# Re-sorting the order list of a one-core attention and spectral-filter kernel by about 700 single moves

## The chip, the cores and the metric

The kernel runs on one core of one Trainium2 chip. The metric is the device time in microseconds (us), lower is better; with one core it is that core's time. The kernel before took 243.63 us at the median of three runs (242.74 to 247.04).

A profile is one recorded execution. Its span is about 2 us shorter than the time of the same run. The array's clock is in the records as a "granted clock", as a share of full speed.

## The reference, cut to what matters

```python
x = A_x                                        # 1 x 2048 x 640, bf16
g = sigmoid((x * gate_w).sum(-1, keepdims=True))
a = A_ref(x, wq, wk, wv, wo, beta)             # memory-augmented attention
b = irfft2(rfft2(x) * (w_r + 1j * w_i))        # spectral filter
out = g * a + (1 - g) * b

# A_ref: 32 heads of 20; 4 segments of 512 tokens, one after the other
for s in range(4):
    p = softmax(qs @ ks.T * scale + causal_mask)
    a_dot = p @ vs
    a_mem = phi(qs) @ M / (phi(qs) @ z + 1e-6)   # memory of earlier segments
    o = sigmoid(beta) * a_mem + (1 - sigmoid(beta)) * a_dot
    M, z = M + phi(ks).T @ vs, z + phi(ks).sum()
# phi(t) = t + 1 where t > 0, else exp(t)
```

## The kernel before

The program is recorded first and ordered second. Every matmul group, vector instruction and DMA is one operation with a number, the operations that it depends on, and the engines that may do it. A hand-tuned list then says in what order the operations stand and, where there is a choice, which engine takes each: value v means operation v // 2 on its engine number v % 2.

```python
def schedule(self, pools, order, nsem=56):
    ...
    for v in order:
        o = ops[v // 2]
        o.eng = list(o.alts)[v % 2]
        queue[o.eng].append(o)
    ...
        # inside head(e): when may the first operation of engine e start?
        if e == "dve" and o.lock:
            t = max(t, free["pool"])
        elif e == "pool":
            t = max(t, port)
```

All that reaches the chip is one queue per engine, in that order, and the semaphores between them. The small simulation in `schedule` only decides which PSUM bank and which semaphore each operation gets. The two branches at the end are its model of how VectorE ("dve") and GpSimd ("pool") hold each other up, with a time called `port`: in the simulation a VectorE operation recorded with `lock` waits until the GpSimd operation in flight is done.

An operation that either VectorE or GpSimd can do is recorded with both costs in nanoseconds (n elements per partition), and the sum of the spectral branch, called `W_add` here, is one of them:

```python
def either(self, fn, n, r, w, prio, name="", after=()):
    return self.Sc.op({"dve": (fn, 67 + 0.52 * n, 68.0), "pool": (fn, 120 + 1.95 * n, 50.0)}, ..., lock=True)

for r, (a0, a1, op) in enumerate(((0, 3, ALU.subtract), (1, 2, ALU.add))):
    fn = lambda e, ...: e.tensor_tensor(Yt.ap(...), Pt.ap(a0 * 322, ...), Pt.ap(a1 * 322, ...), op)
    self.either(fn, KD, ..., name="W_add")          # KD = 321
```

`warm_up` records ten matmuls of 512 columns on a tile of zeros, whose results nothing uses. `phi_max` and `phi_min` make the feature map phi on VectorE. `addmem` (128x640) adds the transposed memory part to the output in the tail and may go to either engine. `m_mask` and the causal masks run on GpSimd. The list of before begins like this:

```python
ORDER = (
    46, 0, 90, 26, 74, 23, 2, 4, 36, 24, 6, 8, 28, 10, 12, 72, 14, 16, 30, 18, 20, 178, ...
    ...            # 2328 entries; 2, 4, ... 20 are the ten warm-ups
)
```

Of the kernel before, what the change touches and what calls it, by code (L numbers as in the profile page):

```python
# [461 lines left out]
class Kern:  # L462
# [79 lines left out]
    def dma(self, dst, src, nbytes, r, w, prio, tr=False, name="", after=(), queue="sp"):  # L542
# [37 lines left out]
        46, 0, 90, 26, 74, 23, 2, 4, 36, 24, 6, 8, 28, 10, 12, 72, 14, 16, 30, 18, 20, 178, 64, 34, 202, 66, 68, 44, 42, 70, 93, 214, 52, 190, 48, 94,  # L580
        204, 97, 216, 180, 192, 218, 104, 98, 182, 76, 206, 101, 194, 38, 208, 220, 196, 103, 198, 222, 201, 184, 224, 186, 210, 188, 296, 50, 212,
        256, 298, 362, 78, 300, 536, 32, 80, 274, 538, 258, 83, 302, 260, 262, 276, 130, 278, 264, 84, 54, 280, 106, 266, 282, 1904, 86, 304, 364,
        284, 88, 366, 108, 380, 306, 576, 132, 826, 268, 290, 828, 814, 110, 368, 578, 831, 816, 113, 382, 384, 386, 819, 370, 540, 388, 832, 270,
        834, 410, 412, 272, 836, 414, 416, 391, 418, 552, 372, 490, 420, 288, 492, 494, 114, 496, 498, 554, 118, 820, 822, 134, 336, 500, 240, 137,
        338, 242, 340, 120, 348, 58, 824, 342, 116, 350, 308, 122, 312, 544, 142, 226, 932, 546, 124, 344, 292, 244, 56, 228, 144, 246, 286, 248, 347,
        139, 352, 230, 294, 232, 126, 250, 354, 146, 234, 374, 1906, 149, 237, 1908, 356, 254, 1910, 359, 2094, 151, 238, 1912, 844, 1914, 252, 2124,
        140, 2126, 1916, 2128, 128, 2130, 360, 166, 2096, 40, 846, 2098, 154, 2132, 848, 2100, 2134, 1924, 326, 1926, 314, 2102, 168, 392, 1928, 2104,
        1930, 156, 892, 310, 1932, 152, 838, 1944, 1934, 170, 334, 1946, 158, 894, 840, 324, 316, 1948, 842, 808, 897, 161, 328, 810, 1950, 1952, 394,
        320, 813, 880, 886, 163, 882, 322, 1954, 888, 560, 332, 502, 884, 504, 396, 506, 330, 172, 508, 890, 448, 376, 510, 1936, 398, 450, 436, 512,
        438, 378, 402, 452, 514, 562, 440, 174, 442, 2162, 400, 1962, 2164, 176, 444, 2166, 516, 556, 454, 456, 2168, 446, 165, 2170, 458, 464, 460,  # L590
        466, 406, 1918, 468, 462, 470, 570, 472, 408, 2172, 910, 912, 542, 474, 898, 900, 318, 914, 602, 903, 2150, 548, 604, 2152, 2154, 2156, 2158,
        1920, 2178, 572, 404, 2160, 1966, 2180, 1958, 2182, 1922, 1968, 574, 904, 60, 2184, 2174, 2186, 906, 594, 2188, 1956, 564, 908, 1970, 2176,
        580, 934, 874, 596, 876, 1972, 879, 476, 566, 1974, 62, 478, 480, 550, 1977, 868, 870, 930, 422, 568, 482, 424, 873, 484, 426, 928, 916, 558,
        486, 428, 430, 488, 918, 2136, 432, 598, 2138, 920, 2140, 434, 2142, 856, 582, 858, 1960, 2144, 922, 519, 861, 924, 606, 584, 2146, 936, 1938,
        520, 2148, 926, 588, 523, 1020, 525, 608, 586, 652, 591, 2596, 802, 654, 862, 850, 804, 864, 852, 1940, 2216, 867, 2204, 2206, 2218, 2208,
        2220, 1942, 2210, 2222, 1980, 854, 2224, 2212, 656, 634, 2226, 2214, 1978, 778, 658, 2006, 2228, 636, 780, 2230, 2008, 1982, 2190, 2010, 782,
        2012, 526, 946, 2014, 786, 784, 2192, 948, 1964, 938, 940, 942, 2194, 788, 950, 2196, 945, 2198, 952, 600, 660, 2017, 2200, 790, 662, 2202,
        792, 2018, 976, 978, 1984, 794, 2020, 958, 798, 796, 1986, 960, 980, 954, 2233, 800, 1988, 982, 610, 956, 664, 2038, 612, 1990, 528, 2236,
        2234, 1992, 965, 530, 984, 986, 2040, 1995, 534, 2076, 988, 2078, 962, 2042, 1996, 2000, 1998, 2044, 991, 614, 618, 1016, 2080, 2024, 620,
        2002, 996, 1014, 2082, 2238, 638, 998, 2084, 972, 2004, 2022, 2046, 622, 668, 974, 992, 624, 2086, 2049, 2056, 626, 1018, 994, 1070, 1072,  # L600
        2058, 1074, 666, 2060, 1022, 1076, 642, 1002, 2050, 806, 1104, 1024, 1026, 670, 645, 1001, 2062, 532, 1028, 2270, 2064, 1031, 628, 2036, 2636,
        2252, 2240, 1106, 2272, 630, 2638, 2274, 2254, 640, 2066, 2276, 2106, 676, 616, 2640, 2256, 678, 592, 2258, 1010, 1004, 2243, 2026, 966, 968,
        2052, 2070, 2028, 1013, 632, 692, 971, 1006, 694, 680, 2244, 2642, 1009, 2644, 686, 1032, 2068, 1034, 682, 2246, 646, 1100, 2054, 2090, 1036,
        2030, 2088, 684, 2288, 649, 710, 2034, 2646, 672, 2290, 1039, 2566, 712, 674, 2292, 2598, 2294, 2600, 2306, 2072, 2602, 2110, 2604, 2308,
        2606, 2074, 2568, 2310, 700, 2092, 2108, 2312, 714, 2608, 726, 2112, 2786, 703, 716, 728, 2114, 1044, 2788, 2570, 688, 1062, 1064, 1046, 2790,
        696, 1066, 2792, 2794, 2650, 1069, 690, 1040, 2796, 650, 2574, 734, 1042, 1110, 698, 1078, 736, 1108, 1082, 730, 1080, 1112, 1114, 1118, 1102,
        1120, 732, 1122, 1116, 750, 1084, 1124, 2260, 2032, 738, 752, 2278, 1049, 2578, 2262, 2280, 2264, 2580, 2282, 704, 2266, 1051, 2284, 2268,
        2296, 2582, 744, 706, 1148, 1150, 2298, 718, 2586, 2648, 754, 2300, 1058, 720, 2302, 3288, 1152, 1089, 2616, 1061, 2618, 1126, 1155, 740,
        1130, 1052, 746, 1132, 1054, 2620, 2572, 1056, 2332, 1086, 1204, 1128, 748, 1206, 2334, 1208, 2622, 2624, 2250, 756, 1096, 1211, 1090, 1135,
        1192, 1092, 2627, 762, 2118, 1095, 2576, 2610, 2390, 1194, 1137, 1098, 1196, 765, 1198, 2392, 1200, 2314, 2120, 2698, 1203, 722, 2700, 2628,  # L610
        1138, 2316, 2702, 2318, 742, 1156, 2122, 1158, 2320, 1160, 1140, 724, 708, 1163, 2704, 2630, 2324, 2612, 2116, 1142, 1168, 2654, 2614, 2706,
        770, 2326, 1170, 1164, 758, 1166, 2842, 2844, 2846, 2848, 761, 2850, 2658, 2652, 2328, 2364, 2852, 766, 2676, 2330, 2366, 2709, 2678, 1280,
# [60 lines left out]
        4000, 4620, 3919, 4514, 4002, 4528, 4634, 4516, 4622, 4004, 4636, 4502, 4506, 4504, 4518, 4509, 4550, 4638, 4530, 4640, 4642, 4532, 4644,  # L673
        4552, 4534, 4647, 4520, 4624, 4522, 4536, 4626, 4525, 4628, 4538, 4562, 4564, 4566, 4568, 4546, 4540, 4630, 4570, 4554, 4633, 4542, 4544,
        4598, 4556, 4600, 4572, 4654, 4648, 4602, 4604, 4575, 4558, 4650, 4652, 4606, 4584, 4561, 4608, 4586, 4588, 4611, 4590, 4582, 4576, 4592,
        4594, 4578, 4580, 4597, 4614, 4616, 4618, 4612,
    )

    def texp(self, s, g, u=None):
# [927 lines left out]
```

## Time and profile before

| | before |
|---|---|
| time, median of 3 runs | 243.63 us |
| profiled span | 240.9 us |
| TensorE busy | 227.4 us (94%) |
| undisturbed matmul steps / tiling changes / TensorE standing | 194.5 / 23.1 / 18.5 us |
| first start of score group 1 of 80 | 12.80 us |
| mean granted clock of that profile | 0.999 |

The prediction below shows the busy list, the chain that ended last, the windows and the waits of this kernel. Two more views belong here, because the experiments turned on them. The first is the timeline of TensorE in the first 12 us (start, length, instruction, how many in one row, and in brackets the idle time before and what ended it).

```profile
1.30 4.17 PE L514 MATMUL psum<-G 128*128 128x512 bf16 x10 [1.30 <-DVE G L797]
5.53 0.61 PE L514 MATMUL psum<-xT,wq 128*32 128x512 bf16 x8
```

The ten warm-up matmuls run without a gap until 5.47 us, and the first projection follows at once. The second is the timeline near the longest standstill, at 207.86 us, with VectorE (DVE), GpSimd (POOL) and TensorE (PE).

```profile
205.67 1.39 POOL L1534 TENSOR_TENSOR oU<-oU,mT 128x640 bf16<-128x640 bf16 x1 [0.40 <-DVE rs L1320]
205.81 1.60 DVE L1534 TENSOR_TENSOR oU<-oU,mT 128x640 bf16<-128x640 bf16 x1
207.33 0.48 DVE L1325 TENSOR_TENSOR on<-psum,rs 128x320 bf16<-128x320 f32 x1
207.86 0.32 PE L514 MATMUL psum<-G,fbg 128*32 128x320 bf16 x4 [1.47 <-DVE on L1325]
```

Two additions of the same size run at the same time on the two engines, and the one on VectorE takes 1.60 us.

### The profile page before, as it was taken

The page shows a single profiled execution, that of the slowest core. Times are in us where ns is not written, and L with a number is a line of the kernel's source. Part 1 is how long each engine was busy: PE and PEld are TensorE (multiplying, and loading weights), DVE is VectorE, ACT ScalarE, POOL GpSimd, SP SyncE. Part 2 cuts the span into 40 slices and gives each one's busy share as a digit, 9 for nine tenths or more (in the row PEclk, how much of TensorE's full clock was granted, in tenths as well). Part 3 has the DMA queues.
Part 4 walks back from the last instruction along what each step waited for, and adds up shares of the span by engine and source line. Part 5 has one row for each costly group of instructions (what it writes and reads, how often), then busy time and mean ns, then how long its engine had stood idle before and what let it go on. Part 6 is the DMA issues. An engine that isn't in the chain of part 4 may idle for free.

```text
span 240.9 us, 10256 instructions
## 1 busy us (share of the span) xinstructions
PE 227.4 (94%) x4361; PEld 140.3 (58%) x4361; DVE 197.5 (82%) x481; ACT 199.5 (83%) x241; POOL 166.7 (69%) x297
## 2 busy tenths in 40 slices
PE   7899999999999999999989999999999999799994
PEld 2574566765456566555546655455545467567794
DVE  0579998889899996898999798998988896946563
ACT  2289687899899999999889989999999988698730
POOL 8514259447969856937982999895989868579730
PEclk9999999999999999999999999999999999999999
DMA  7999849995996774582779663354765995882123
GB/s 168 278 363 214 225 130 185 244 207 147 243 253 156 158 222 129 141 239 68 232 206 246 189 179 111 102 125 155 205 207 163 243 216 87 121 106 86 57 87 109
DMA packets 58928, 42.17 MB, mean 175 GB/s; under 512 B 30020, under 2 KB 55172, under 8 KB 58884
## 3 DMA queue, kind: packets, MB, share of 16 engines
q1 hardware_dynamic: 57844, 40.96, 69.5%
q8 instruction: 34, 0.56, 1.0%
q10 hardware_dynamic: 1040, 0.57, 0.8%
q14 instruction: 10, 0.08, 0.1%
HBM read 23.32 MB, written 12.30 MB: 148 GB/s over the span
## 4 chain that ended last, share of the span: by engine, by line
PE 52%; DVE 17%; DMA 10%; ACT 9%; SPq 8%; issue 3%; DVEq 0%
PE psum L514 47%; ACT ex L1263 6%; SPq L548 5%; PE psum L512 5%; DMA xsb<-in_A_x_dram 3%; DMA r_scr<-rc 3%; SPq L546 2%; DMA pkn<-phk 2%; DVE Pt L1439 2%; DVE G L1485 1%; DVE xf L901 1%; DVE oU L1526 1%; DVE xsb L906 1%; ACT et L1072 1%; DVE ub L525 1%
## 5 line engine op out<-in xcount | busy, mean ns | idle before, releaser
L1263 ACT ACTIVATE ex<-psum 128x2048 bf16<-128x2048 f32 (+4 forms) x92 | 138.7, 1507 | 13.8 <-PE psum L514 12.1
L1284 POOL TENSOR_SCALAR_AFFINE_SELECT ex<-ex 128x256 bf16<-128x256 bf16 (+2 forms) x224 | 122.3, 568 | 38.0 <-ACT ex L1263 34.5
L514 PE MATMUL psum<-xT,wk 128*128 128x256 bf16 (+1 forms) x280 | 34.0, 273 | 0.8 <-DMA wk<-in_A_wk_dram 0.8
L514 PE MATMUL psum<-qkp 20*64 20x64 bf16 (+5 forms) x1280 | 32.5, 270 | 2.0 <-ACT ex L1263 1.5
L514 PE MATMUL psum<-xT,wq 128*128 128x512 bf16 (+1 forms) x135 | 30.7, 380 | 0.5 <-DMA xT<-in_A_x_dram 0.4
L514 PE MATMUL psum<-wv,xT 128*32 128x321 bf16 (+3 forms) x400 | 30.0, 301 | 0.5 <-DVE va L1115 0.3
L1439 DVE TENSOR_TENSOR Pt<-psum,Wt 128x642 bf16<-128x642 f32 x32 | 25.5, 821 | 2.3 <-PE psum L514 1.9
L514 PEld LDWEIGHTS psum<-qkp 20*64 20x64 bf16 x1280 | 13.5, 103 | 19.4 <-ACT ex L1263 13.6
L514 PEld LDWEIGHTS psum<-xT,wk 128*128 128x128 bf16 (+1 forms) x280 | 19.9, 97 | 7.0 <-DMA wk<-in_A_wk_dram 0.9
L512 PE MATMUL psum<-wo,oU 128*32 128x320 bf16 x480 | 21.7, 300 | 0.0
L906 POOL TENSOR_TENSOR xsb<-xf 128x320 bf16<-128x320 bf16 (+2 forms) x12 | 9.1, 762 | 17.1 <-DVE xsb L906 13.3
L514 PEld LDWEIGHTS psum<-wv,xT 128*32 128x32 bf16 (+1 forms) x400 | 14.3, 96 | 8.3 <-issue 2.2
L1115 DVE TENSOR_TENSOR va<-psum,ebx 128x320 bf16<-128x320 f32 x32 | 15.2, 483 | 4.7 <-PE psum L514 2.2
L514 PE MATMUL psum<-big,Ac 128*128 128x160 bf16 (+2 forms) x96 | 18.1, 258 | 0.5 <-DVE Pt L1439 0.3
L514 PE MATMUL psum<-big,Cp 128*128 128x321 bf16 (+1 forms) x96 | 18.0, 302 | 0.2 <-DVE G L1485 0.2
L514 PE MATMUL psum<-ex,va 128*32 128x64 bf16 (+3 forms) x576 | 17.4, 256 | 0.7 <-DVE dn L1152 0.3
L525 DVE CAST ot<-psum 128x320 bf16<-128x320 f32 x21 | 10.0, 490 | 9.6 <-PE psum L512 6.1
L1485 DVE TENSOR_TENSOR G<-eo,psum 128x320 bf16<-128x320 f32 x32 | 14.7, 482 | 3.6 <-PE psum L514 2.6
L514 PEld LDWEIGHTS psum<-ex,va 128*32 128x32 bf16 x576 | 11.1, 96 | 9.7 <-POOL ex L1284 3.4
L514 PE MATMUL psum<-tt,Yt 128*128 128x256 bf16 (+1 forms) x96 | 16.4, 275 | 0.2
L1072 ACT ACTIVATE et<-qu 128x512 bf16<-128x512 bf16 x25 | 15.6, 629 | 0.2
L512 PEld LDWEIGHTS psum<-wo,oU 128*32 128x32 bf16 x480 | 12.0, 96 | 4.3 <-issue 1.1
(99 smaller groups left out, 392.8 us busy)
## 6 DMA issues: line engine op xcount, KB each, us to landing
qkp<-qk_scr SPq DMA_DIRECT2D x28, 160.0 KB
tt<-tab_tt SPq DMA_DIRECT2D x8, 512.0 KB, 4.1
qk_scr<-qu SPq DMA_DIRECT2D x12, 256.0 KB, 3.1
u_scr<-ub SPq DMA_DIRECT2D x12, 256.0 KB, 3.6
xsb<-in_A_x_dram SPq DMA_DIRECT2D x8, 320.0 KB, 7.2
oU<-u_scr SPq DMA_DIRECT2D x15, 128.0 KB, 3.1
out_dram<-ot SPq DMA_DIRECT2D x12, 160.0 KB
Wt<-in_B_w_r_dram SPq DMA_DIRECT2D x16, 80.2 KB, 2.6
```

What stands on the lines that cost most here:

```text
L512: h = e.matmul(dst, wt, r_, start=st, stop=sp_, **{**kw, "tile_position": (0, q), "skip_group_check": True})
L514: h = e.matmul(o_, l_, r_, start=st, stop=sp_, **kw)
L525: alts["dve"] = (lambda e: e.tensor_copy(dst(), src()), 67 + 1.04 * n, 68.0)
L546: return e.dma_start_transpose(d_, s_)
L548: return e.dma_start(d_, s_)
L906: self.either(lambda e, dst=dst, src=src, d0=d0, n=n, op=op: e.tensor_tensor(xs.ap(o + dst, [D, 2], [1, n]), xf.ap(src + d0, [321, 2], [1, ...
L1072: self.one("act", lambda e: e.activation(et.ap(0, [1, L]), qsl(), ACT.Exp), L, [qb], [b("et", pi_)], late, name="phi_exp")
L1115: self.one("dve", lambda e: e.tensor_tensor(va.ap(i * H * VW + h0 * VW, [VW, nh], [1, DH]), self.ps(bank, 0, [DH, nh], [1, DH]), self.ebx. ...
L1263: self.one("act", lambda e, d=d, q=q: e.activation(self.ex.ap(*d), self.ps(bank, *q), ACT.Exp, scale=SC), n, [bank], [self.exb(s, 2 * pr + ...
L1284: self.one("pool", lambda e: e.affine_select(self.ex.ap(e0 + d0, [1280, 4], [1, n], np_=np_), self.ex.ap(e0 + s0, [1280, 4], [1, n], np_=np_),
L1439: self.one("dve", lambda e, ri=ri, Pt=Pt, Wt=Wt, wo_=wo_, bank=bank: e.tensor_tensor(Pt.ap(ri * 322, [644, 2], [1, KD]), self.ps(bank, 0, ...
L1485: self.one("dve", lambda e, q=q, n2=n2, bank=bank, eo=eo: e.tensor_tensor(self.G.ap(n2 * D + 639 * q, [1 - 2 * q, 320]), eo.ap(q, [1, 320] ...
```

## The change

The intent was to shorten a simulated time: some 700 single moves of one operation in the list, each kept only where a model with measured times of transfers became shorter by a larger step. No operation, size or SBUF buffer changed; the diff is only the numbers of the list. The PSUM banks follow from the order, though: when the two lists are run through `schedule`, 1041 of the 1572 operations that use a bank get another one.

```diff
     ORDER = (
-        46, 0, 90, 26, 74, 23, 2, 4, 36, 24, 6, 8, 28, 10, 12, 72, 14, 16, 30, 18, 20, 178, 64, 34, 202, 66, 68, 44, 42, 70, 93, 214, 52, 190, 48, 94,
-        204, 97, 216, 180, 192, 218, 104, 98, 182, 76, 206, 101, 194, 38, 208, 220, 196, 103, 198, 222, 201, 184, 224, 186, 210, 188, 296, 50, 212,
+        25, 0, 90, 26, 74, 2, 23, 4, 36, 6, 8, 28, 10, 12, 72, 14, 46, 190, 30, 16, 18, 64, 66, 34, 68, 42, 202, 70, 44, 20, 52, 214, 48, 178, 204,
+        93, 192, 180, 182, 206, 94, 194, 38, 216, 97, 196, 184, 208, 76, 186, 98, 210, 104, 101, 188, 218, 213, 198, 220, 362, 201, 103, 222, 296, 50,
         ... (about 190 further changed lines of the same kind)
```

Read as queues, the head changes as follows: the first key weights go out on ScalarE's queue (value 25 instead of 24), and TensorE's queue starts with seven warm-ups, projection 95, warm-ups 8 and 9, projection 101, warm-up 10, where before all ten warm-ups stood together. 46 operations change engine, among them seven `W_add` from GpSimd to VectorE and two the other way.

## The prediction

> **What bounds the kernel now.** The first view is the page's busy list, read together with the chain that ended last.
>
> ```profile
> PE 227.4 (94%) x4361; PEld 140.3 (58%) x4361; DVE 197.5 (82%) x481; ACT 199.5 (83%) x241; POOL 166.7 (69%) x297
> ...
> PE 52%; DVE 17%; DMA 10%; ACT 9%; SPq 8%; issue 3%; DVEq 0%
> PE psum L514 47%; ACT ex L1263 6%; SPq L548 5%; PE psum L512 5%; DMA xsb<-in_A_x_dram 3%; DMA r_scr<-rc 3%; SPq L546 2%; DMA pkn<-phk 2%; DVE Pt L1439 2%; DVE G L1485 1%; DVE xf L901 1%; DVE oU L1526 1%; DVE xsb L906 1%; ACT et L1072 1%; DVE ub L525 1%
> ```
>
> TensorE is busy almost throughout and is half of the chain; the rest of the chain is small pieces of all other engines. Busy is too coarse, because overlapping matmuls count whole. So I took the start times of the 4361 matmuls from the trace, grouped them by the 1073 matmul groups of the program (their order is known), and measured the distance from one group's first start to the next one's. Undisturbed groups are very regular: 216 ns for 512 columns of a projection, 136 ns for four 320-column output pieces side by side, 557 ns for an attention-times-values group. The sum of these undisturbed distances is 194.5 us. Where the array's tiling (whole, four column strips, or the 4 by 2 pieces of the scores) differs between neighbours, 101 ns are added, very evenly; there are 229 such changes, 229 x 0.101 = 23.1 us. The first matmul starts at 1.3 us and the last ends 3.2 us before the span's end. What is left, 240.9 - 194.5 - 23.1 - 1.3 - 3.2 = 18.8 us (18.5 when summed group by group), is TensorE standing. Only 29 of these standstills are over 0.2 us and they make 11.8 us; the rest are crumbs.
>
> The windows view shows where they are (columns: window and its length, then busy us and instruction count of PE, PEld, DVE, ACT, POOL, then clock, DMA share and GB/s).
>
> ```profile
> 0.00:12.00 12.00, 9.44 (x134) 4.68 (x135) 3.56 (x7) 2.83 (x5) 8.82 (x13) 1.00 0.89 222
> 12.00:38.00 26.00, 25.13 (x341) 15.98 (x340) 24.17 (x60) 21.10 (x33) 10.03 (x16) 1.00 0.88 231
> 38.00:69.00 31.00, 30.52 (x514) 19.17 (x508) 27.27 (x66) 27.60 (x37) 21.92 (x44) 1.00 1.01 209
> ...
> 101.00:125.00 24.00, 22.28 (x390) 12.61 (x389) 22.16 (x56) 22.52 (x26) 17.92 (x36) 1.00 0.66 182
> ...
> 180.00:208.00 28.00, 25.91 (x618) 15.62 (x609) 23.88 (x62) 24.27 (x30) 22.05 (x36) 1.00 0.82 171
> 208.00:238.00 30.00, 29.67 (x900) 22.37 (x892) 17.91 (x44) 19.09 (x24) 18.37 (x31) 1.00 0.40 91
> ```
>
> TensorE loses 2.6 us in the first 12 us (first loads), 1.7 us at 101 to 125, 2.1 us at 180 to 208, and almost nothing in the last 30 us, which are solid TensorE work. That last row matters most: a standstill removed anywhere before 208 us brings the solid stretch, and the end, forward by its own length. Who causes the standstills, from the list of waits (total us, times, longest):
>
> ```profile
> PEld psum L514 <- ACT ex L1263: 13.6, 45, 0.8
> PEld psum L514 <- POOL ex L1284: 4.2, 13, 0.5
> PEld psum L514 <- DVE Pt L1439: 3.8, 15, 0.6
> ...
> PE psum L514 <- DVE on L1325: 1.5, 1, 1.5
> ```
>
> The weight-load waits overlap running matmuls, so they are not all lost, but they rank the causes: the exponentials that free the four score banks, then the masks, then banks that VectorE frees. The longest single standstill, 1.5 us at 207.86, is put down to VectorE; the chain shows what had held VectorE (start, length, what):
>
> ```profile
> 194.42 6.75 DMA r_scr<-rc
> 201.19 2.30 DMA r<-r_scr
> 203.51 2.01 DVE oU L1526 x5
> 205.64 0.25 DVE rs L1323
> 205.89 1.52 DVE oU L1534
> 207.41 0.41 DVE on L1325
> 207.86 0.32 PE psum L514 x4
> ```
>
> A 32 KB store takes 6.75 us because it queues behind five 128 KB loads and a transposing load issued just before it.
>
> [...]227.4 us busy against 217.6 us of undisturbed work and tiling changes. [...]here the maximum of the feature map takes 433 ns at the median while GpSimd works and 283 ns otherwise[...].
>
> **The change part by part.** Only the order list differs: no operation, size, buffer or address pattern changes. Comparing the two queues of each engine (longest common order), 156 of 1073 matmul groups, 80 of 460 VectorE operations, 49 of 276 GpSimd, 6 of 242 ScalarE and 82 of 231 SyncE issues have really moved, median distance zero to two places on TensorE and SyncE. About 40 operations change engine. So it is a fine polish, with the large structure kept; the 80 score groups are in the same order.
>
> Work moved: ScalarE takes five net operations, mostly PSUM evictions of 0.54 to 0.60 us; with the rows' durations its load is +2.5 us. VectorE gives up evictions of about 0.68 us and takes 5 net additions of the spectral part at about 0.33 us each, sum -0.2 us. GpSimd loses those 5 at 0.73 us and two others near 1 us, -5.6 us. TensorE's 194.5 us stay; tiling changes go from 229 to 240, +11 x 0.101 = +1.1 us. Eight of the eleven lie before the first score group, where warm-up matmuls are now mixed with the first projections as filler while loads are awaited, so they cost little; three, 0.3 us, are in solid work.
>
> Start: the first key weights now go out on ScalarE's queue and the first transposed load is SyncE's first issue rather than its second. The waits at 6.59 and 7.62 us (0.63 and 0.59 us of standstill) should shrink; I put the stage at -0.3 us net of filler.
>
> Tail chain: the transposing load before the 6.75 us store goes behind it, another goes earlier, and the multiplication that makes the stored data moves ahead of two 0.49 us VectorE sums. The five loads still stand in front. From the standstill of 1.5 us I take off 1.0 us.
>
> Middle: after 1.6 us for the start and 1.5 us for the tail, 11.8 - 3.1 = 8.7 us of larger standstills remain. They are single collisions (a bank freed late, a mask late, a transposed load late), just what single moves can cure. My choice is that a third goes, -2.9 us, and new ones worth +1.0 us appear, because the moves were picked on calculated times and not on the chip. The heavier ScalarE costs something where exponentials release the score banks: +0.3 us.
>
> Sum: -0.3 - 1.0 - 2.9 + 1.0 + 0.3 + 0.3 = -2.6 us, from 243.6 to 241.0 us.
>
> **The rivals.** First, that the moves fit the model only: standstills below 0.2 us change with small timing differences, and 240 tiling changes are paid for sure. Then removed and new waits cancel and the time is 243 to 245 us. For it speaks that 6.7 of the 18.5 us are crumbs that no order aims at; against it, that the ends of the queues are hardly disturbed. Second, that the model is close to the chip: then two thirds of the 11.8 us go, about -7 us plus 1 us of new ones and switches, 237.5 us. For it speaks the regularity of the 216, 136 and 101 ns steps; against it, DMA landings that spread (one and the same kind of 32 KB store took 6.75 us here). Third, ScalarE becomes the bound: it has 83% plus 2.5 us, and its exponentials need 1.88 us each with TensorE waiting; then some 2 us come back and the time stays near 244 us. Its idle time before exponentials, 13.8 us in the groups view, speaks against that.
>
> **Range and chances.** The floor with no standstill is 1.3 + 194.5 + 23.1 + 3.2 = 222 us, so 2% (4.9 us) needs more than a quarter of all standstill removed net; I give that 0.20. A loss of 2% would need 5 us of new standstill in a hardly changed structure: 0.04. The 8 in 10 range is 237.5 (second rival) to 244.5 us (first and third).
>
> **What would show it.** Right: the last stretch of about 30 us stays solid; TensorE's standstill by the same sum falls from 18.5 to about 15 us; the wait near 207 us shrinks below 0.8 us with the small store landing in under 5 us; the first score group comes at or before 12.8 us; busy ScalarE rises and GpSimd falls as computed. Wrong: standstill unchanged with other owners (first rival), or standstill near 11 us (second), or the waits of weight loads on exponentials well above 13.6 us (third).

## The result, and the profile after

The changed kernel took 245.5 us at the median of four runs (245.05 to 245.87). The kernel before, beside it, took 243.19 us at the median of four (241.8 to 247.04). Executions over 1.5% slower than the fastest of the same kernel are left out of the means. A ratio in this document is the mean time of one kernel's runs over the mean of the other's runs of the same rounds, so it is not quite the ratio of the medians. Here it is 1.0105, with a 95% interval of 1.0057 to 1.0153. That is a small loss, within 2%, where 241.0 us was predicted; the time lies 1 us above the predicted range.

The busy list and the chain of the kernel after are these.

```profile
PE 229.2 (94%) x4348; PEld 140.5 (58%) x4361; DVE 197.3 (81%) x484; ACT 201.7 (83%) x245; POOL 160.7 (66%) x290
...
PE 63%; ACT 17%; DVE 7%; POOL 5%; DMA 4%; issue 3%; DVEq 0%; ACTq 0%; POOLq 0%
PE psum L514 56%; ACT ex L1263 13%; PE psum L512 7%; POOL ex L1284 3%; DMA xT<-in_A_x_dram 2%; DMA qk_scr<-qu 2%; POOL Yt L1444 1%; DVE Yt L1444 1%; ACT et L1072 1%; ACT qu L523 1%; DVE G L1485 1%; ACT Cp L523 1%; DVE phk L1085 1%; DVE Bt L525 1%; DVE ub L525 1%
```

ScalarE gains 2.2 us and GpSimd loses 6.0 us, about as computed (x4348: 13 matmul records are missing from this trace). The chain is now mostly TensorE; the store of the small reciprocals is gone from it, and the spectral additions (Yt, L1444) have come in. The same windows as in the prediction:

```profile
0.00:12.00 12.00, 9.42 (x94) 3.56 (x98) 1.89 (x6) 1.51 (x2) 7.67 (x12) 1.00 0.89 217
12.00:38.00 26.00, 25.75 (x370) 16.17 (x365) 23.08 (x58) 21.16 (x32) 9.68 (x14) 1.00 0.87 233
38.00:69.00 31.00, 28.79 (x476) 18.36 (x476) 26.64 (x63) 27.98 (x42) 20.97 (x43) 1.00 0.86 196
...
101.00:125.00 24.00, 22.77 (x375) 12.88 (x376) 22.14 (x55) 23.00 (x27) 17.37 (x35) 1.00 0.80 179
...
180.00:208.00 28.00, 26.89 (x580) 15.70 (x581) 24.22 (x64) 24.84 (x30) 22.09 (x39) 1.00 0.75 178
208.00:238.00 30.00, 29.99 (x918) 22.39 (x918) 19.43 (x50) 22.07 (x28) 18.53 (x32) 1.00 0.42 89
```

In the first window TensorE is as busy as before (9.42 against 9.44 us) but has finished 94 matmuls instead of 134: busy time hides that they were slow. From 38 to 69 us it now stands 2.2 us instead of 0.5. From 180 to 208 us it stands 1.1 us instead of 2.1, and the last 30 us are solid in both.

The cleanest comparison uses the 80 score groups, whose order is the same in both kernels. Their start times are milestones (us):

| start of | before | after | difference | step |
|---|---|---|---|---|
| score group 1 | 12.80 | 14.95 | +2.15 | |
| score group 13 | 59.55 | 61.06 | +1.51 | start: +1.5 |
| score group 25 | 91.85 | 95.28 | +3.43 | middle: +1.9 |
| score group 65 | 187.24 | 190.92 | +3.68 | +0.3 |
| last TensorE group | 237.36 | 240.02 | +2.66 | tail: -1.0 |

By the same sum as in the prediction, undisturbed steps stay at 194.5 us, tiling changes go from 23.1 to 24.2 us, and standing goes from 18.5 to 20.0 us. The time went in two places, the start and a stretch near 60 to 92 us, and the tail gave 1.0 us back.

**The start.** The first 12 us of TensorE in the kernel after:

```profile
1.30 3.17 PE L514 MATMUL psum<-G 128*128 128x512 bf16 x7 [1.30 <-DVE G L797]
5.74 0.62 PE L514 MATMUL psum<-xT,wk 128*32 128x256 bf16 x8 [1.27 <-DMA xT<-in_A_x_dram]
6.29 1.03 PE L514 MATMUL psum<-G 128*128 128x512 bf16 x2
7.26 0.62 PE L514 MATMUL psum<-xT,wq 128*32 128x512 bf16 x4
7.81 0.61 PE L514 MATMUL psum<-G 128*128 128x512 bf16 x1
```

The seven warm-ups end at 4.47 us, then TensorE idles 1.27 us for the first transposed load. That load was issued earlier than before (0.78 us instead of 1.25) but landed later (5.61 instead of 5.40 us). And the array is still slow at 7 us: the steps of 512 columns in this trace are 0.43 us until 10.31 us and 0.22 us afterwards, while before they reached 0.22 us at 5.05 us. So the first projections run at half rate, and the three warm-ups meant as filler take 0.43 us each in front of them. The third transposed load, too, was issued earlier (4.62 instead of 4.95 us) and landed later (9.33 instead of 8.66 us).

**The middle.** Near 63 us the kernel after shows this on VectorE, GpSimd and TensorE:

```profile
62.77 2.07 DVE L1444 TENSOR_TENSOR Yt<-Pt 128x321 bf16<-128x321 bf16 x2
62.64 0.47 POOL L1361 TENSOR_TENSOR Mz<-Macc,hm 128x154 bf16<-128x154 f32 x1
63.07 2.62 POOL L1284 TENSOR_SCALAR_AFFINE_SELECT ex<-ex 128x256 bf16<-128x256 bf16 x5
64.77 0.68 DVE L525 CAST ub<-psum 128x512 bf16<-128x512 f32 x1
65.50 0.35 PE L514 MATMUL psum<-Mz,phq 128*128 128x154 bf16 x3 [1.03 <-DVE ub L525]
```

Two spectral additions stand one behind the other on VectorE (the change moved the first there; the second was there before) and take 2.07 us together, while GpSimd works through a row of six instructions. Only when they are over does VectorE empty a PSUM bank (ub), and TensorE has been idle 1.03 us for it. How unusual that is shows in the durations of this line on VectorE, first before, then after (minimum, median, maximum in ns).

```profile
L1444 DVE TENSOR_TENSOR Yt<-Pt x16: 313/320/604, 57.2 to 162.8; 128x321 bf16<-128x321 bf16 x16
```

```profile
L1444 DVE TENSOR_TENSOR Yt<-Pt x21: 310/325/1173, 58.8 to 166.2; 128x321 bf16<-128x321 bf16 x21
```

The median is the same; the longest has doubled. Three of the 21 take 0.98, 1.17 and 1.17 us (at 62.77, 63.67 and 85.36 us), each beside three GpSimd instructions. None of the three is over when one GpSimd instruction is done; each lasts through parts of several in a row, and that is what the scheduler's two lines about `port` do not have. The sum of such extra time on VectorE is not larger than before (counted above the median of the same line, tiles and shape, 11.6 us before and 10.5 after), but after it falls where TensorE waits for a bank.

### The profile page after: what moved, and what is told of

Its sections match the earlier page's. It is cut to its first block, busy times and chain, and to the rows that moved or that the text cites.

```text
span 243.8 us, 10253 instructions
## 1 busy us (share of the span) xinstructions
PE 229.2 (94%) x4348; PEld 140.5 (58%) x4361; DVE 197.3 (81%) x484; ACT 201.7 (83%) x245; POOL 160.7 (66%) x290
## 4 chain that ended last, share of the span: by engine, by line
PE 63%; ACT 17%; DVE 7%; POOL 5%; DMA 4%; issue 3%; DVEq 0%; ACTq 0%; POOLq 0%
PE psum L514 56%; ACT ex L1263 13%; PE psum L512 7%; POOL ex L1284 3%; DMA xT<-in_A_x_dram 2%; DMA qk_scr<-qu 2%; POOL Yt L1444 1%; DVE Yt L1444 1%; ACT et L1072 1%; ACT qu L523 1%; DVE G L1485 1%; ACT Cp L523 1%; DVE phk L1085 1%; DVE Bt L525 1%; DVE ub L525 1%
## 5 line engine op out<-in xcount | busy, mean ns | idle before, releaser
L514 PE MATMUL psum<-xT,wk 128*128 128x256 bf16 (+1 forms) x280 | 34.5, 285 | 1.3 <-DMA xT<-in_A_x_dram 1.3
L514 PE MATMUL psum<-xT,wq 128*128 128x512 bf16 (+1 forms) x122 | 27.7, 408 | 1.0 <-DVE dn L1152 0.4
L514 PEld LDWEIGHTS psum<-xT,wk 128*128 128x128 bf16 (+1 forms) x280 | 19.4, 99 | 9.7 <-issue 4.9
L906 POOL TENSOR_TENSOR xsb<-xf 128x318 bf16<-128x318 bf16 (+2 forms) x12 | 9.6, 805 | 16.5 <-DVE xsb L906 11.6
L514 PE MATMUL psum<-big,Ac 128*128 128x321 bf16 (+2 forms) x96 | 18.2, 257 | 1.0 <-DVE Pt L1439 0.4
```

Of the source, the lines that this page charges most:

```text
L514: h = e.matmul(o_, l_, r_, start=st, stop=sp_, **kw)
L906: self.either(lambda e, dst=dst, src=src, d0=d0, n=n, op=op: e.tensor_tensor(xs.ap(o + dst, [D, 2], [1, n]), xf.ap(src + d0, [321, 2], [1, ...
```

## The experiments

The theory (V) after the result: the start costs 1.5 us because the warm-up matmuls are split and the array stays at half rate; the middle costs 2 us because spectral additions moved to VectorE wait behind rows of GpSimd instructions; the tail gains 1 us by its DMA order. The rivals: many small shifts without one place (first rival of the prediction), the order of TensorE or of the loads itself, and for the tail a collision of additions instead of the store. All hybrids below have the same operations, and each queue was spliced from the two kernels' queues. An edit of the order can move PSUM banks as well: e2, e6, e8, e10 and e12 keep every bank of the kernel that they edit, but e3 changes the bank of 457 of the 1572 operations, e7 of 492 and e11 of 497 (against e10), so those three edit more than their diffs show. "The first eight" (e1 to e8) ran on one chip, with before at 244.87 us at the median; e9 to e12 on another, with before at 244.41; e13 to e16 on the first again, with before at 245.15.

### e1_head_before: before's order for the first 13 us

```diff
 every queue of the changed kernel:
-    changed order from the first operation
+    before's order for what before starts in its first 13 us, then the changed order
```

> The changed order, but everything that the kernel before started in its first 13 us (up to the first score group) stands as there, on all engines. The first score group started at 12.8 us before and at 14.95 us after the change. Theory A (TensorE's start costs and part of it is carried to the end): the first score group returns to about 12.8 us and the end comes 1.0 to 1.5 us earlier than in the changed kernel, ratio to before 1.005. Rival B (the first 38 us are set by loads and folds, so the start is absorbed, and the loss comes from 60 to 115 us): the first score group returns, but the end stays, ratio 1.010.

Measured: 244.65 us, ratio 0.9996 (0.9946 to 1.0045). In its trace score group 1 starts at 13.52 us and group 13 at 60.35 us, against 14.95 and 61.06 in the kernel after. Theory A's direction came, with a ratio even below its 1.005. Group 1 scatters: the eleven traces whose queues have before's order up to 13 us have it between 12.77 and 13.52 us, 12.98 at the median, so e1 has a late one of these and before's 12.80 is an early one. The loss up to group 1 is in the first 13 us; the middle still loses, 94.57 us at group 25 against 91.85 before.

### e2_warm_first: only the ten warm-ups together again

```diff
 TensorE's queue of the changed kernel:
-    warm 1-7, projd 95, warm 8, warm 9, projd 101, warm 10, projd 107, projd 89, ...
+    warm 1-10, projd 95, projd 101, projd 107, projd 89, ...
```

> The changed order with one thing undone: the ten warm-up matmuls stand together at the head of TensorE's queue again; loads and all other orders stay changed. Theory A1 (the mixed warm-up leaves the array at half rate for the first projections, and the last three warm-ups stand in the way of real work): the 512-column steps of the first projections return from 0.43 to 0.22 us, the first score group comes at 12.6 to 13.2 us. Rival A2 (the load order is what delays it): the steps may be fast, but the first score group stays near 14.5 us because the projections wait for inputs. End: as in the run with the old head, 1.0 to 1.5 us below the changed kernel if the start carries, 0 if not.

Measured: 245.51 us, 1.0032 (0.9987 to 1.0077). The array is at full rate from 4.66 us, and group 1 starts at 14.03 us, 0.9 us earlier than in the kernel after and 1.2 us later than before. The expected 12.6 to 13.2 us was missed. At full rate TensorE now stands 1.12 us at 9.45 us for a transposed load and 0.82 us at 12.19 us for key weights. e6 below, with the warm-ups split and full rate from 4.07 us, has group 1 at 14.20 us. So without the half rate the changed start is still about 1.1 us behind the median of 12.98, and with it (14.36 to 15.06 us in the traces of after, e9 and e3) 0.2 to 0.9 us more. The larger share lies in the changed order of loads and projections; these are single traces, and the load order was not tried alone.

### e3_adds_back: three spectral additions back on their old engines

```diff
-VectorE: ... W_mul 497, W_add 500, W_add 501, ...   and   ..., W_add 567, ...
+VectorE: ... W_mul 497, W_add 501, ...              and   W_mul 566, W_add 543, ...
+GpSimd:  ... m_mask 403, W_add 500, ...             and   ..., W_add 567, W_add 568, ...
```

> The changed order with three of the spectral additions back on the engine they had before: two return from VectorE to GpSimd at their old places, one from GpSimd to VectorE. In the changed kernel the additions on VectorE near 63 and 85 us took 0.98, 1.17 and 1.17 us instead of 0.32. Theory C [...]: the slow ones vanish, the standstills of 1.2 us at 65.5 and 0.5 us near 88 us shrink, the end comes 1.0 to 2.0 us earlier than in the changed kernel. Rival D (the standstills there follow from the shifted start or from GpSimd's lateness with masks): additions are fast but the end moves by less than 0.5 us.

Measured: 246.52 us, 1.0071 (1.0024 to 1.0119): a miss, it did not get faster. The trace shows why, on VectorE, GpSimd and TensorE:

```profile
62.88 3.06 DVE L1444 TENSOR_TENSOR Yt<-Pt 128x321 bf16<-128x321 bf16 x1
62.74 0.48 POOL L1361 TENSOR_TENSOR Mz<-Macc,hm 128x154 bf16<-128x154 f32 x1
63.18 0.73 POOL L1444 TENSOR_TENSOR Yt<-Pt 128x321 bf16<-128x321 bf16 x1
63.87 2.44 POOL L1284 TENSOR_SCALAR_AFFINE_SELECT ex<-ex 128x256 bf16<-128x256 bf16 x5
66.59 0.35 PE L514 MATMUL psum<-Mz,phq 128*128 128x154 bf16 x3 [2.03 <-DVE ub L525]
```

The one addition left on VectorE now takes 3.06 us, ten times its usual 0.32, beside seven GpSimd instructions, the first six of them without a gap; it ends at 65.94 us, just after the first gap (0.06 us at 65.78). Moving one of the two made GpSimd's row longer and the other addition wait through it. This is the strongest sight of such a wait, though the experiment as a cure failed (and it moved banks, too). A second thing showed in the windows of the same trace (columns as in the prediction; the granted clock is the third number from the end):

```profile
65.18:68.59 3.41, 1.43 (x32) 0.89 (x34) 3.31 (x11) 2.17 (x4) 1.24 (x4) 1.00 0.72 205
68.59:72.00 3.41, 3.41 (x28) 1.36 (x29) 2.72 (x7) 2.45 (x3) 3.34 (x7) 0.50 0.42 115
```

After a stretch of 3.41 us in which TensorE was busy for only 1.43 us, the array ran at half rate for exactly 3.41 us. Such a stretch lowers the mean granted clock of the run by 3.41 / 2 / 245 = 0.007, so it reads 0.993, and two of them would by the same sum read 0.986 (e13's trace below, with 6.83 us, reads 0.984). Five of the six runs of e3 read 0.993 or less.

### e4_tail_after and e5_cut93: before's order up to 187 us, or up to 93 us

```diff
 every queue:
+    before's order for what before starts before 187 us (e4) or 93 us (e5)
     then the changed order
```

> The kernel before up to 187 us, then the changed order for all that is left. Theory E (the tail part of the change is a gain by itself, 1.2 us between 197 and 209 us in the traces): 1.0 to 1.3 us below the kernel before, ratio 0.995, with the standstill of 1.5 us before the last output stretch gone. Rival F (the tail only gained because it came late and its transfers had more time): ratio 1.000.

> The order before up to 93 us, the changed order from there. The run with the old head alone had ratio 0.9996, the run with the old order up to 187 us 0.9909. Their traces differ by about 1.9 us between 60 and 93 us and by little after. Theory M (the middle loss lies at 60 to 93 us): ratio 0.991 to 0.993, like the run cut at 187 us. Rival N (the loss is spread over 93 to 187 us): ratio near 0.998.

Measured: e4 242.66 us, 0.9909 (0.9863 to 0.9956); e5 242.43 us, 0.9905 (0.9862 to 0.9948). The changed tail alone is worth 0.9% of 244.9, about 2.2 us, twice the expected 1.0 to 1.3 us; e15 below shows why. The changed stretch from 93 to 187 us costs nothing, since e5 has it and e4 has not. And e1 and e5 differ only between 13 and 93 us: the middle costs 244.65 - 242.43 = 2.2 us.

### e6_adds_pool: both additions at 63 us on GpSimd

```diff
-VectorE: ... W_mul 497, W_add 500, W_add 501, ...   and   ..., W_add 567, ...
+VectorE: ... W_mul 497, ...                         and   W_mul 566, W_add 543, ...
+GpSimd:  ... m_mask 403, W_add 501, W_add 500, ...  and   ..., W_add 567, W_add 568, ...
```

> The changed order, but both spectral additions near 63 us on GpSimd (one behind the other, in front of its run of masks), and those near 85 us as in the earlier run that moved three. That earlier run left one addition on VectorE, which took 3.06 us beside seven GpSimd operations in a row, and TensorE stood 2.2 us. Theory P [...]: with nothing on VectorE to starve, the standstill near 65 us falls below 0.6 us from 1.2 us in the changed kernel, and the end comes 1.0 to 2.0 us earlier than there, ratio to before 1.003. Rival Q (GpSimd becomes late by the two additions of 0.73 us, masks and the values product wait): end unchanged or later, ratio 1.010.

Measured: 243.72 us, 0.9965 (0.9913 to 1.0018), faster than the kernel after's 1.0105. The standstill near 88 us went, as expected, and so did the one in front of the matmul that stood 1.03 us in the kernel after (psum<-Mz,phq):

```profile
62.82 1.41 POOL L1444 TENSOR_TENSOR Yt<-Pt 128x321 bf16<-128x321 bf16 x2
63.36 0.69 DVE L525 CAST ub<-psum 128x512 bf16<-128x512 f32 x1 [0.87 <-PE psum L514]
64.11 0.35 PE L514 MATMUL psum<-Mz,phq 128*128 128x154 bf16 x3
65.29 0.32 PE L514 MATMUL psum<-qkp 20*64 20x64 bf16 x24 [0.83 <-ACT ex L1263]
```

Near 65 us 0.83 and 0.39 us stayed, where under 0.6 was expected. The trace puts the first down to an exponential that frees a score bank (ACT ex), and the second to a product that stood behind the minimum of the feature map (phi_min), which ran beside a row of masks and took 1.13 us. This run's array reached full rate at 4.07 us, with the split warm-ups, so part of the gain in time can come from the start. The distance from score group 13 to 25 leaves the start out: 32.30 us before, 34.22 after (34.22 in e9 and e1, 34.23 in e2), 35.60 in e3 and 32.77 in e6 (traces with the same order in this stage agree to 0.03 us, except that e10, with before's order there, has 33.14). With every bank as in the kernel after, the additions' place alone gives back 1.45 of the 1.92 us, in one trace.

### e7_tail_swap: e4, with one maximum moved back

```diff
 VectorE's queue of e4:
-    ... mem_rec 1492, phi_max 1652, mem_den 1500, mem_rec 1501, mem_mul 1493, ...
+    ... mem_rec 1492, mem_den 1500, mem_rec 1501, mem_mul 1493, phi_max 1652, ...
```

> The run with the old order up to 187 us and the changed tail, with one VectorE operation moved behind another: the maximum near 123.7 us, which took 1.20 us instead of 0.28 because GpSimd was in an unbroken run of masks, now stands behind the multiplication that frees the bank TensorE waits for. TensorE's standstill there was 0.99 us. Theory P [...]: standstill below 0.3 us and the end 0.5 to 0.9 us earlier than in the run without the move, ratio 0.988. Rival: the next operations of VectorE inherit the wait, end unchanged at 0.991.

Measured: 241.62 us, 0.9881 (0.9836 to 0.9925), the fastest of all at the median and faster than both kernels, though within 2% of before. The same place in e4 (before's order there), then in e7:

```profile
120.50 4.28 POOL L1284 TENSOR_SCALAR_AFFINE_SELECT ex<-ex 128x256 bf16<-128x256 bf16 x8 [0.47 <-ACT ex L1263]
123.72 1.20 DVE L1084 TENSOR_SCALAR phq<-qu 128x512 bf16<-128x512 bf16 x1
125.69 0.45 PE L514 MATMUL psum<-Bt,tt 128*128 128x321 bf16 x2 [0.83 <-DVE mem L1157]
```

```profile
122.36 0.43 DVE L1157 TENSOR_TENSOR mem<-psum,dn 128x320 bf16<-128x320 f32 x1
122.70 0.70 DVE L1084 TENSOR_SCALAR phq<-qu 128x512 bf16<-128x512 bf16 x1
122.98 0.44 PE L514 MATMUL psum<-Bt,tt 128*128 128x321 bf16 x2
```

In e4 the maximum waits through GpSimd's row of masks, and the product (mem) that frees TensorE's bank stands behind it. In e7 the product goes first and TensorE has no idle time in front of the same matmul. One move, chosen because a slowed instruction (1.20 us, against a usual 0.28) stood in front of a bank release, gave 1.0 us in the median and 0.7 us in the mean of six runs. The intervals of e4 and e7 overlap, so the times alone do not show it. In the traces the distance from group 25 to 65 is 94.90 to 95.13 us in the three runs with this move (e7, e11, e12) and 95.14 to 95.86 in the six with before's order there, about 0.4 us apart at the medians. The move also changed banks elsewhere.

### e8_warm_mixed: before, with the warm-ups split as in the change

```diff
 TensorE's queue of before:
-    warm 1-10, projd 89, projd 101, ...
+    warm 1-7, projd 89, warm 8, warm 9, projd 101, warm 10, ...
```

> The kernel before with one part of the change alone: three of its ten warm-up matmuls stand between the first four projection steps, as in the changed kernel; loads and everything else as before. Theory A1 (the interrupted warm-up keeps the array at half rate): 512-column steps of 0.43 us until about 10 us, first score group 1.0 to 2.0 us later than with the old head (12.8 to 13.5 us), end 0.8 to 1.5 us later, ratio 1.004. Rival (the slow steps came from the changed loads): steps at 0.22 us, first score group at most 0.5 us later, ratio 1.000.

Measured: 244.42 us, 0.9966 (0.9913 to 1.002): no loss. In its trace the array is at full rate from 4.34 us and group 1 starts at 12.79 us, as in before. So splitting the warm-ups did not by itself cost time here. The moment of full rate varies from trace to trace, and what sets it is not shown: with split warm-ups, e6 and e8 had full rate at 4.07 and 4.34 us, while after, e9 and e3 had it at 10.31, 9.01 and 10.56 us. With the ten together, 12 of 13 traces had it by 7.2 us.

### e9_after_again: the kernel after, unchanged, on the other chip

```diff
 (no edit)
```

> The changed kernel once more, unaltered, beside the experiments and on their chip, since the first measurement was on another. It should again take 1.5 to 3.0 us more than the runs of before at full granted clock, ratio 1.004 to 1.010; the first measurement was 1.0105. [...]the step time of the first projections can be 0.22 us in this trace.

Measured: 245.9 us, 1.0072 (1.0031 to 1.0114). All six runs have a clock of 0.999 or 1.0; group 1 starts at 14.36 us, group 25 at 95.20, the last TensorE group at 240.28. The loss is reproduced.

### e10_pair: two additions of the tail exchanged between the engines

```diff
 queues of before:
-VectorE: ... pv_rec 1914, addmem 2080, pv_mul 1915, pv_den 1870, pv_rec 1871, pv_mul 1872, ...
-GpSimd:  ... mask512c 1928, addmem 2178, ...
+VectorE: ... pv_rec 1914, pv_mul 1915, pv_den 1870, pv_rec 1871, pv_mul 1872, addmem 2178, ...
+GpSimd:  ... mask512c 1928, addmem 2080, ...
```

> The kernel before with one pair of operations exchanged: of the two additions of 640 columns near 206 us, the one that stood on VectorE and took 1.60 us beside the other on GpSimd goes to GpSimd, and the other goes to VectorE, two products later. All transfers stay. Theory P [...]: the standstill falls below 0.5 us, the half-rate windows late in the kernel vanish (granted clock 1.00 in most runs instead of 0.993), ratio 0.990 to 0.994. Rival R (the prediction's reason, the store that lands 6.75 us after its issue): the standstill stays at 1.0 us or more, ratio 1.000.

Measured: 242.59 us, 0.9943 (0.9904 to 0.9981). The loads and stores are untouched, and the standstill at that matmul goes from 1.47 us to nothing that the view prints:

```profile
205.88 0.49 DVE L1325 TENSOR_TENSOR on<-psum,rs 128x320 bf16<-128x320 f32 x1
206.43 0.32 PE L514 MATMUL psum<-G,fbg 128*32 128x320 bf16 x4
208.85 0.18 PE L514 MATMUL psum<-qkp 20*64 20x64 bf16 x1 [0.80 <-issue]
207.22 0.48 DVE L1534 TENSOR_TENSOR oU<-oU,mT 128x640 bf16<-128x640 bf16 x1
```

The addition on VectorE takes 0.48 us when GpSimd's addition is over, instead of 1.60. So, as theory P had it, the collision of the two additions made that standstill; the store chain, to which the prediction gave it, is the same in both (VectorE waits some 0.5 us for its reload before and in e10). But TensorE now stands 0.80 us a little later, at 208.85 us, after the next pair of additions has run side by side on the two engines, and from score group 69 to 77 e10 takes 21.78 us, the trace of before 21.48. What e10 gains is clock: with two shorter pauses (0.19 and 0.80 us) in place of the long one, all six runs read 0.999 or 1.000. That is nearly all of its gain, since its runs (242.03 to 243.64 us) are no faster than the three runs of before that read 0.998 or more (242.38 to 243.09 us). The expected ratio of 0.990 to 0.994 was just missed.

### e11_pair_swap and e12_pair_wka: e10 with the moved maximum, and with the key weights on ScalarE's queue as well

```diff
 e11, VectorE's queue of e10:  phi_max 1652 behind mem_mul 1493, as in e7
 e12, queues of e11:
-SyncE:   ..., ld_beta, ld_wka, xT 14, ...
+ScalarE: ld_wqa, ld_wka, ...
```

> The exchanged pair, and the maximum near 122 us behind the multiplication that TensorE waits for. Three operations differ from the kernel before. Theory P: another 0.5 to 0.9 us below the exchanged pair alone, ratio 0.987 to 0.991, as good as the run with the changed tail and the same move (0.9881). If the changed tail had other merits, it is 0.3 us or more behind that run.

> The same three, and the first key weights issued from ScalarE's queue behind the first query weights, as the changed kernel has them on that queue. It frees 0.43 us of SyncE before the second and third transposed load. If the start is set by SyncE's issues: first score group 0.3 to 0.6 us earlier, end 0.2 to 0.5 us earlier than without. If it is set by the transfers themselves: no change within 0.2 us.

Measured: e11 241.79 us, 0.9915 (0.9879 to 0.9951); e12 242.41 us, 0.9912 (0.9871 to 0.9954). e11 is 2.6 us below its before, e7 3.2 us below its own. The intervals overlap, but the traces agree with a difference: from group 65 to the last TensorE group e11 takes 49.80 us and e7 49.09. So three moves in before's list give most of what e7 gives, and the changed tail seems to have some 0.6 us of other merit, as the expectation's last sentence had it. In e11, too, a further addition on VectorE (at 206.98 us) takes 0.91 us beside one on GpSimd. Issuing the key weights from ScalarE, which takes an issue of 0.42 us (at 3.13 us in the trace of before) off SyncE's queue, gains nothing: group 1 starts at 13.92 us, in the one trace with contiguous warm-ups that reached full rate late (9.93 us). There too the first transposed load came late, and TensorE paused from the end of the warm-ups to 6.70 us.

### e13_mid_vectors and e14_mid_tensor: which engines' order loses the middle?

Both have before's order up to 13 us and the changed one after 93 us, and between these they mix.

```diff
 between 13 and 93 us:
+e13: VectorE, GpSimd, ScalarE as before; TensorE, SyncE as changed
+e14: TensorE, SyncE as before; VectorE, GpSimd, ScalarE as changed
```

> Before's order up to 13 us and the changed order after 93 us on all engines, as in both the run of before's head (244.65 us, 0.9996, the middle changed) and the run cut at 93 us (242.43 us, 0.9905, the middle as before). Between 13 and 93 us VectorE, GpSimd and ScalarE keep before's order and engine choices, TensorE and SyncE take the changed ones. Theory V (the middle's 2.2 us are lost where VectorE additions wait behind rows of GpSimd instructions): near the run cut at 93 us, ratio 0.988 to 0.994, the standstill near 65 us under 0.5 us, first-to-25th score group distance near 78.5 us instead of 81.1. Rival T (the loss is in the order of TensorE's own groups or of the loads): near the other run, 0.997 to 1.002. If both orders are needed to fit each other, this one is slower than both.

> The complement: between 13 and 93 us TensorE and SyncE keep before's order, VectorE, GpSimd and ScalarE take the changed one with its engine choices. Theory V: the loss stays, ratio 0.997 to 1.002 and a standstill of about 1 us near 65 us. Rival T: the loss goes, 0.988 to 0.994. Mixed: slower than both.

Measured: e13 245.92 us, 1.0063 (1.0025 to 1.01); e14 247.41 us, 1.0134 (1.009 to 1.0179). e14 is slower than either parent, e1 (0.9996) and e5 (0.9905). e13 is slower than e5; against e1 it is not clear, since the intervals overlap and its trace holds 6.83 us at half rate (clock 0.984; its three runs at 1.000 take 245.4 to 245.5 us). Neither theory's number came, and e13 leans to rival T's side: TensorE's and SyncE's changed orders lose without the moved additions. The third line of the expectation fits best: the orders belong together, and a mix loses anew. So the middle's 2.2 us cannot be given to one group of engines by this test. What stays as evidence for the additions is what the traces of after and e3 show at 63 to 66 us, and e6's 1.45 us between groups 13 and 25.

### e15_before_look and e16_before_look2: where does before lose its clock?

```diff
 (no edit: the list of before written out again, the same queue on every engine)
```

> The kernel before with its list written out again, the same queue on every engine, for one more profile. So far its trace exists only at a mean granted clock of 0.999, while most of its other runs had 0.993. If 0.993 comes again, the theory of the half-rate window says: one stretch of 3.41 us at clock 0.50, and it begins within 3.5 us after the standstill of 1.5 us at 208 us. Rival: it lies elsewhere (at 124 us, or in the first 13 us), and then the changed tail is not what cures it.

> The same once more, since a single look shows the half-rate window only in about four of five runs. Same expectation: at 0.993 the stretch at clock 0.50 follows the standstill at 208 us, at 0.986 there is a second one, which would most likely follow the standstills at 122 to 126 us; at 1.00 none.

Measured: single runs, whose state is therefore unknown, 243.69 and 244.5 us, at clocks 0.993 and 0.992. Both show the standstill near 208 us and a stretch of 3.41 us at half rate next to it: in e15 from 208.51 us, 1.2 us after TensorE resumed, in e16 from 207.61 us, before it resumed at 207.98. The windows of e15, and then of the earlier trace of the same kernel, whose clock was 0.999:

```profile
205.10:208.51 3.41, 1.95 (x82) 1.44 (x82) 3.34 (x8) 1.79 (x3) 1.69 (x2) 1.00 0.51 74
208.51:211.92 3.41, 3.41 (x62) 1.69 (x54) 2.14 (x5) 1.77 (x4) 2.00 (x4) 0.50 1.19 169
211.92:215.33 3.41, 3.41 (x96) 2.35 (x100) 0.61 (x2) 3.10 (x3) 1.30 (x3) 1.00 0.41 94
```

```profile
205.10:208.51 3.41, 1.94 (x62) 1.64 (x63) 3.31 (x8) 2.04 (x2) 1.55 (x2) 1.00 1.11 103
208.51:211.92 3.41, 3.41 (x116) 2.15 (x112) 2.82 (x7) 2.92 (x5) 2.30 (x4) 1.00 0.72 156
```

The same pause (1.95 and 1.94 us busy of 3.41) went with a half-rate stretch in one execution and with none in the other: 62 matmuls against 116 in the next 3.41 us. What decides is not shown. The stretches of e15 and e16 begin a whole number of steps of 3.413 us after their first moment of full rate (7.12 and 6.22 us), 59 in both, which is also where the step's size is taken from (201.39 / 59); e3's stretch fits it with 17, from 10.56 to 68.59 us; counted so, a step of the earlier trace begins at 206.44 us, with the pause at its very start. The busy share of the step before does not decide: e16's half rate followed 2.41 us busy of 3.42. Between score groups 69 and 77 the two slow-clock traces stand 1.5 us (e15) and 1.4 us (e16) longer than the earlier one. So before seems to lose 1.4 to 1.5 us there in most runs: 31 of the 34 timed runs of before in the three batches have a clock below 0.995, and none of the ten runs of the kernel after has.

## Why the prediction was wrong

**The start, predicted -0.3 us, measured +1.5 us.** The failing step is that the eight extra tiling changes and the warm-up matmuls "cost little" as filler while loads are awaited, and that the waits for loads "should shrink". (Counted on the two queues, six and not eight of the eleven extra changes stand before the first score group.) The warm-ups were not filler. The load landed 0.2 us later although it was issued 0.5 us earlier, TensorE idled 1.27 us with its warm-ups used up, and at the half rate that followed the three remaining warm-ups stood in front of the projections. e2 gave back 0.9 us of the 2.15 at the first score group, and before's whole head (e1) 1.4 us. With full rate early, e2 and e6 still have the first score group some 1.1 us late, so the later loads are the larger part and the half rate, which came in some of these traces and not in others, 0.2 to 0.9 us. Two traces with split warm-ups escaped it, three did not, and the load order was not tried alone in the changed kernel.

**The middle, predicted -2.9 + 1.0 + 0.3 us, measured about +2 us.** The milestones give +1.9 us (60 to 92 us), and e1 against e5 gives 2.2 us for 13 to 93 us. The step "a third goes" has nothing to show for it: of the two longest old standstills one, 0.83 us at 124.34, did go (no more than 0.30 us is left in one piece between 102 and 148 us), but from group 25 to 65 nothing was gained (95.64 us after, 95.39 before, and either order scatters by half a microsecond), because others took its place (0.58 us at 180.24). The other, at 207.86, belongs to the tail. And the new ones were put at half their size. The prediction knew that VectorE is slower beside GpSimd, from the maximum's 433 instead of 283 ns, but took it as a modest lengthening. In the runs it is a wait through whole rows of GpSimd instructions, up to 3.06 us for 0.32 us of work. The seven additions that moved to VectorE were entered as 0.33 us each; two of them, and one that stood there already, took 0.98 to 1.17 us, and TensorE waited for what stood behind two of these. e6 shows the size: the additions' place alone is 1.45 of the 1.92 us between groups 13 and 25. The failed cure of e3 agrees. e13 and e14 show that it is not the only thing that can lose it: the fit of all queues was lost. The simulation in `schedule`, whose wait at `port` lasts one instruction, misses this stage: run on the lists off the chip, it puts it only 0.4 us longer in the kernel after, where the traces have 1.9, and in e6 0.6 us longer still, where the trace has 1.45 less. Nothing speaks against the +0.3 us for a heavier ScalarE, and no run measures it: its load rose by 2.2 us, and weight loads waited on exponentials 14.0 us instead of 13.6.

**The tail, predicted -1.0 us.** In the traces it is -1.0 us, in part by luck, and in the times it is more. The failing step is the reason: "the chain shows what had held VectorE", the store that lands late. e10 leaves that chain as it was and the standstill goes, so the collision of two additions made it. In the kernel after the two additions are apart. The reload of the small store landed at 203.49 us before and at 206.26 after, which is 6.60 and 5.57 us after the start of score group 69, so the prediction's earlier data did come 1.0 us earlier against the work around it, and VectorE no longer waited for it. But TensorE's own groups near there were re-ordered as well, and curing the collision alone (e10) did not shorten the stage. So the -1.0 us in the traces is not given to one of these. And the prediction did not see that the standstill in most runs, going by their clocks and the traces of e15 and e16, comes with a half-rate stretch, which cost 1.4 to 1.5 us in those two traces: that was missing from the one trace it read, whose clock was 0.999. With it, e4's 2.2 us for the tail is 1.0 us from the traces and some 1.2 us, an estimate by difference, of clock.

**The sum.** +1.5 + 2.2 - 2.2 = +1.5 us, which is about what the second chip shows (245.9 - 244.41). The first rival, moves that fit the model only, came nearest with 243 to 245 us, but its reason (crumbs and tiling changes) was not it: of the +2.66 us in the traces, tiling changes are 1.1 us, half of them in the start, and the rest has the addresses above. The second rival (a good model) and the third (ScalarE as the bound) fall.

**What was right.** Loads by engine, 240 tiling changes, a solid last 30 us, and no large change in either direction. Of the marks named beforehand, standing did not fall to 15 us (20.0), and the first score group did not come by 12.8 us (14.95); the wait near 207 us did shrink below 0.8 us. Whether the small store landed in under 5 us the trace of after does not say: nothing waited for it alone.

**What stays open.** The load order of the start, never tried alone; the remaining 0.5 us of the middle, and why e13's and e14's mixes lose as much as they do; what in the changed tail gives the 1.0 us; what the moved PSUM banks add; and when a pause costs clock.

## What to carry to other kernels

Look for instructions that take several times their own median and ask what stood behind them: here moving one slowed VectorE instruction (1.20 us, against a usual 0.28) behind the one that frees a TensorE bank gave 0.3% of the mean on top of the tail (not clear of the noise in the times, some 0.4 us in the traces), and three such moves in the old list (e11) beat all 700 of the search. Before running what a search on a model has found, ask a second model: the simulation inside the kernel, run on both lists, gives 236.1 us for before and 239.4 for after, a loss of 3.3 us where the traces have 2.7. It has the start (1.5 us at group 13) but only 0.4 of the 1.9 us in the middle, where its wait at `port` is for one instruction instead of a row, and it is no oracle: it puts e5 and e7 behind before as well, and they were faster. The search used another model, which is not on record, so whether its moves gathered at the same weak line is not shown. And compare mean clocks before comparing times: in two traces of before a pause of about 1.5 us came with a further loss of 1.4 to 1.5 us at half rate, and in a third trace of the same kernel it did not. The mean clock does not count the half rate at the start: e9's profile reads 1.000 although its steps were slow until 9.01 us.
